# Reciprocals of the softmax sums, broadcast by four transfers per quad instead of one

## The chip, the cores and the metric

The kernel runs on one core of one Trainium2 chip. The metric is the device time of one execution in microseconds. Three runs of the kernel before gave 896.04, 896.61 and 898.95 us; the median is 896.61 us.

## What is computed

One transformer block over 2048 tokens of 512 columns, conditioned by a vector `c`: six rows of shift, scale and gate come out of `c`, then attention with 32 heads of 16 columns, then a gated feed-forward layer of 1792 columns.

```python
mod = (_silu(c) @ w_mod).reshape(c.shape[0], 6, 1, -1)          # sa, ca, ga, sb, cb, gb
h = _layernorm(x) * (1 + ca) + sa
qkv = (h @ wqkv) ...                                              # 32 heads, 16 columns each
scores = jnp.einsum('bhqd,bhkd->bhqk', q, k) * 16 ** (-0.5)
o = jnp.einsum('bhqk,bhkd->bhqd', _softmax(scores), v)
x = x + ga * (o @ wo)
h = _layernorm(x) * (1 + cb) + sb
x = x + gb * ((_gelu(h @ w_gate) * (h @ w_up)) @ w_down)
```

The softmax divides by a sum over the keys. The change touches only the path by which the reciprocals of these sums reach the vector engine.

## The kernel before

The kernel is written out by a recorder. The methods of `_Recorder` (`mm`, `act`, `tt`, `ts`, `dma` and so on) put each operation on one of five in-order queues: PE (matrix), ACT (scalar), DVE (vector), POOL, and SP, which issues nearly all transfers. `rec` (line 169) works out which semaphores an operation has to wait for, from the bytes that it reads and writes, and `emit` (line 381) writes the queues out. A planner (`stream`, line 1097) decides the order while recording. It keeps an own estimate of the times (`model`, line 246; a transfer there occupies SP for 450 ns) and always takes what its estimate says is ready. So the order of all five queues depends on the estimated cost of each operation: an edit that changes these costs changes the order of other work too.

**Attention.** The queries are cut into six sets (`SETS`, line 31): three of 512 queries, one of 256 and two of 128. The heads are taken four at a time; four heads of one set are called a quad here (a unit in the code), and there are eight quads for each set, except that the last two sets share their first five quads. PE computes scores into `ps_sc` (`qk`, line 1342), ACT takes their exponentials into `E`, one to three tiles of 512 columns in one instruction (line 1286), and PE multiplies them with the values into `ps_pv` (`pv_mms`, line 1354). The values have a 17th column of ones, so that the sum of the exponentials comes out as a 17th row of each head: a quad occupies rows 32j to 32j+16 of the 128, j from 0 to 3, with the sum in row 32j+16. Part of the exponentials is not computed on ACT: DVE makes them out of the scores with integer arithmetic, into `dreg` or `mreg` (line 1293), and four shifted copies of each (`shift_task`, line 1366). The planner decides which rounds go there (lines 1261 to 1275), four score tiles at a time.

**End of a quad.** `unit_end` (line 1388) copies `ps_pv` to `osb` (128 rows, 512, 256 or 128 columns, f32). Then a chain of steps follows: the four rows of sums go to DRAM (`scr_den`), come back spread over 128 rows (`den`), DVE takes the reciprocals (`rden`), these go to DRAM (`scr_rec`), and one transfer brings them back as `rb`, each head's row of reciprocals repeated over its 32 rows (line 1408). `fin2` (line 1411) multiplies `osb` by `rb` into `onorm`, which the output projection (`wo`) reads. Rows 32j+16 to 32j+31 of `wo` are zero, so that only rows 32j to 32j+15 of `onorm` count. Of the 43 quads' ends, 39 go through this chain; quads 6 and 7 of the last two sets take another way (`near_end`, line 845), by PE and a reciprocal on DVE.

**Steps and queues.** The steps of the chain form one task: the planner puts each step on its queue as soon as its estimate says that it can start, and the next step only after that. SP holds, besides these steps, the loads of the feed-forward weights (256 KB each, lines 897, 902 and 794 to 804) and the stores of the output. The feed-forward layer and the projections run between the attention work as side work (`plan`, line 1022), on PE, DVE and a little on ACT. PE also runs matmuls that only keep it busy (`ps_sc<-xs,ident` and `ps_mi<-xs,ident`, lines 1258 and 1330).

The prologue (line 496) loads the inputs, zeroes or fills some tiles on POOL and DVE, normalises the first four tiles of tokens and starts the attention.

Of the kernel before, what the change touches and what calls it, by code (L numbers as in the profile page):

```python
# [17 lines left out]
DH = 16  # L18
# [398 lines left out]
class _Kernel(_Recorder):  # L417
# [78 lines left out]
    def prologue(self):  # L496
        sp, act, pe, dve, pool = "sp", "act", "pe", "dve", "pool"
        xv = self.A_x.rearrange("b (t p) d -> p (b t) d", p=P)
        wmv = self.w_mod.rearrange("(a p) n -> p a n", p=P)
        wqv = self.A_wqkv.rearrange("(a p) (k n) -> p a k n", p=P, k=3)  # L500
        wq4 = self.wqkv.rearrange("p a (k n) -> p a k n", k=3)
        self.dma(sp, self.xs[:, 0:2, :], xv[:, 0:2, :], "x0")
        self.dma(act, self.crow[0:1, :], self.c, "c")
        self.dma(act, self.xs[:, 2:4, :], xv[:, 2:4, :], "x1")
        for i in range(2):
            self.dma(sp, self.wmod[:, :, D * i:D * i + D], wmv[:, :, D * i:D * i + D], "wm%d" % i)
        for k in (1, 0):
            self.dma(act, wq4[:, :, k, 0:P], wqv[:, :, k, 0:P], "wq%d" % k)
        self.dma(sp, self.xs[:, 4:8, :], xv[:, 4:8, :], "x2")
        self.dma(sp, wq4[:, :, 2, 0:P], wqv[:, :, 2, 0:P], "wq2")  # L510
        for i in range(2, 4):
            self.dma(sp, self.xs[:, 4 * i:4 * i + 4, :], xv[:, 4 * i:4 * i + 4, :], "x%d" % (i + 1))
        for k in range(3):
            self.dma(sp, wq4[:, :, k, P:D], wqv[:, :, k, P:D], "wr%d" % k)
        self.dma(sp, self.wmod[:, :, 1024:3072], wmv[:, :, 1024:3072], "wm2")

        self.memset(dve, self.warm, 0.0)
        self.memset(dve, self.ones, 1.0)
        self.memset(dve, self.pv[:, :], 0.0)
        self.memset(dve, self.scp[:, SC - 1, :], 0.0)  # L520
        self.warm_up(7)
        self.memset(pool, self.ident[:, :], 0.0)
        self.affine_select(self.ident[:, :], [[-1, P]], ALU.not_equal, 1.0, 0, 1)
        self.memset(pool, self.rm4, 1.0)
        self.affine_select(self.rm4, [[-32, 4]], ALU.is_ge, 0.0, -16, 1)
        self.affine_select(self.rm4, [[32, 4]], ALU.is_ge, 0.0, 31, -1)
        self.reduce(self.rm[:, 1:2], self.rm4, mybir.AxisListType.X, ALU.add)
        self.ts(dve, self.rm[:, 0:1], self.rm[:, 1:2], -1.0, 1.0, ALU.mult, ALU.add)
        self.memset(pool, self.vaug[:, :, :].rearrange("p t (h c) -> p t h c", c=VW)[:, :, :, DH:VW], 1.0)

        for dc in range(NDC):
            self.mm(self.scp[:, 0, dc:dc + 1], self.crow[0:1, P * dc:P * dc + P], self.ones[0:1, 0:1])
        self.act(self.tcol[:, :], self.scp[:, 0, 0:NDC], ACT.Tanh, scale=0.5)
        self.ln_stat(0)
        self.ln_stat(1)
        self.stt(self.tcol[:, :], self.tcol[:, :], 1.0, self.scp[:, 0, 0:NDC], ALU.add, ALU.mult)
        self.ts(dve, self.sc_bf[:, :], self.tcol[:, :], 0.5, None, ALU.mult)
        self.warm_up(6)
        self.mod_cols(self.scp[:, 1, 0:8], 0, range(4))
        self.warm_up(6)  # L540
        self.ln_stat(2)
        self.ln_stat(3)
        self.ln_rstd(0, 4)
        self.mod_cols(self.scp[:, 1, 0:8], 0, range(4, 8))
        self.warm_up(2)
        nb = self.nwt[:, 0:4]
        self.stt(nb, self.mv[:, 0:4, 0], -1.0, self.rstd[:, 0:4], ALU.mult, ALU.mult)
        for t in range(4):
            dst = self.tb1[:, 0, t, :]
            if t % 2 == 0:  # L550
                self.ln_norm(t, dst)
            else:
                self.act(dst, self.xs[:, t, :], ACT.Identity, bias=nb[:, t:t + 1], scale=self.rstd[:, t:t + 1])
        self.copy(dve, self.modA[:, :], self.scp[:, 1, 0:8])
        self.ts(dve, self.modA[:, 4:8], self.modA[:, 4:8], 1.0, None, ALU.add)
        pts = [self.scp[:, 2 + dc, :].bitcast(BF16)[:, 0:512] for dc in range(3)] + [self.mi[:, :].bitcast(BF16)[:, 0:512]]
        for t in range(4):
            for dc in range(NDC):
                self.transpose(pts[dc][:, P * t:P * t + P], self.tb1[:, 0, t, P * dc:P * dc + P], self.ident[:, :])
        for dc in range(NDC):  # L560
            self.modulate(dve if dc % 2 == 0 else act, self.hT[:, dc, 0:512], pts[dc], self.modA, dc)
        self.ln_stat(4)
        self.proj_q(0, 0, self.scp[:, 3, :], act)
        kb = self.scp[:, 4, :]
        self.proj(kb, 512, 0)
        for e in range(2):
            self.ts(dve, self.km[e][:, 0, 0:512], kb, self.rm[:, e:e + 1], None, ALU.mult)
        for t in range(5, 8):
            self.ln_stat(t)
# [818 lines left out]
    def unit_end(self, u, acc):  # L1388
        sets, qd, q0, W = u
        b, lo, hi = self.osb_span(u)  # L1390
        osb, rb = self.osb[:, lo:hi], self.rb[:, lo:hi]
        assert not self.blocked(u)
        self.copy("dve", osb, acc[:, 0:W])
        if sets[0] >= len(SETS) - 2 and len(sets) == 1 and qd >= 6:
            self.done(("osb", sets[0], qd))
            return
        self.live[u] = (lo, hi)
        m = 4 * W // P
        o = 8 if BCOL[sets[0]] else 0
        sem = b + 4 * (o > 0)  # L1400
        s1, s2 = self.scr1[b, P * o:P * o + 4 * W], self.scr2[b, P * o:P * o + 4 * W]
        den, rden = self.den[:, b, o:o + m], self.rden[:, b, o:o + m]
        steps = [
            ("sp", lambda: self.dma("sp", s1.rearrange("(j n) -> j n", j=4), self.osb[DH:P:32, lo:hi], "da%d" % sem)),
            ("sp", lambda: self.dma("sp", den, s1.rearrange("(p n) -> p n", p=P), "db%d" % sem)),
            lambda: self.recip(rden, den),
            ("sp", lambda: self.dma("sp", s2.rearrange("(p n) -> p n", p=P), rden, "dc%d" % sem)),
            ("sp", lambda: self.dma("sp", rb,
                                    s2.rearrange("(j o n) -> j o n", j=4, o=1).broadcast_to([4, 32, W]), "dd%d" % sem))]

        def fin2():
            c = OCOL[sets[0]]
            self.tt("dve", self.onorm[:, qd, c:c + W], osb, rb, ALU.mult)
            if self.probing is None:
                self.live.pop(u)
                for k in sets:
                    self.done(("onorm", k, qd))

        def free():
            c = OCOL[sets[0]]  # L1420
            return ("den", u) in self.have and all(
                ("wo", k) in self.have for k in range(sets[0]) if OCOL[k] < c + W and c < OCOL[k] + SETS[k][1])
        self.task(steps, ("den", u))
        self.task([fin2], None, free)
# [148 lines left out]
```

## Time and profile before

| what | value |
|---|---|
| median of three runs | 896.61 us (896.04 to 898.95) |
| the profiled execution | 895.94 us, span 894.1 us, mean granted clock 0.992 |
| busy, share of the span: PE, ACT, DVE, POOL | 91%, 94%, 76%, 0% |
| transfers | 47.64 MB, mean 53 GB/s |

The span runs from the first to the last instruction of the profile; the execution around it is 1.84 us longer. Engines are PE, ACT, DVE, POOL and SP as above, PEld the loading of weights into PE, and "SPq" SP's issuing of transfers. A row of the timeline gives the start and the duration in us, the engine, the line, the operation, what it writes and reads, how many such instructions, and in brackets how long the engine stood idle before it and what ended that. A row of the groups gives an instruction by its shape, its count, its busy time in us and the mean ns of one, and the idle time before it. A row of waits gives the waiting engine and its line, what it waited for, the total us, the times and the longest one. Most operations are recorded by a helper, so that their line is that of the helper; they are told apart by their tiles.

### The profile page before, as it was taken

Reading aid. Unit: us, or ns where it says so; the run is one execution under the profiler, and the core shown is the slowest. Engines: PE = TensorE matmul, PEld = TensorE weight load, DVE = VectorE, ACT = ScalarE, POOL = GpSimd, SP = SyncE. Lnnn points to the kernel's source line nnn. Section 1 sums busy time; section 2 is a strip of 40 time slices with the busy share of each in tenths; the row PEclk is TensorE's granted clock in tenths of the full one; section 3 lists DMA queues with packets and bytes.
Section 4 is the critical chain, followed back from the end, with each engine's and each line's share of the span. In section 5 each row is a group of like instructions: output and inputs, shape, how many; then the busy total and the mean of one; then the engine's idle time right before and its main releaser. Section 6 shows DMA issues by size and latency. Waiting matters only on the chain.

```text
span 894.1 us, 27778 instructions
## 1 busy us (share of the span) xinstructions
PE 811.9 (91%) x12637; PEld 284.9 (32%) x12642; DVE 680.8 (76%) x1288; ACT 843.9 (94%) x740; POOL 3.7 (0%) x11
## 2 busy tenths in 40 slices
PE   7899899989998998999999899999988889988887
PEld 3333232322222222223322222223433333344355
DVE  7745689988998888998888999989846672655264
ACT  5999999999999999999999999999989999999982
POOL 1000000000000000000000000000000000000000
PEclk9999999999999999999999999999999999999999
DMA  9000000000003101211003121110003321663300
GB/s 305 2 26 23 8 15 12 18 14 15 3 26 85 49 26 39 60 49 37 27 1 95 40 61 37 49 50 15 28 27 102 85 80 38 173 198 91 101 7 13
DMA packets 73115, 47.64 MB, mean 53 GB/s; under 512 B 15369, under 2 KB 69318, under 8 KB 72998
## 3 DMA queue, kind: packets, MB, share of 16 engines
q1 hardware_dynamic: 71668, 45.34, 17.2%
q8 instruction: 99, 1.62, 0.7%
q10 hardware_dynamic: 1330, 0.53, 0.2%
q14 instruction: 18, 0.15, 0.1%
HBM read 43.25 MB, written 2.61 MB: 51 GB/s over the span
## 4 chain that ended last, share of the span: by engine, by line
ACT 57%; PE 26%; DVE 8%; DMA 6%; issue 1%; SPq 0%; ACTq 0%; DVEq 0%
ACT E L324 55%; PE ps_mi L311 10%; PE ps_sc L311 10%; PE ps_pv L311 6%; DMA rb<-scr_rec 4%; ACT wreg L324 2%; DVE dreg L336 1%; DMA scr_rec<-rden 1%; DVE st L364 1%; DVE onorm L328 1%; DMA xs<-in_A_x_dram 1%; DVE osb L345 1%; DVE mreg L336 0%; DVE wreg L328 0%; DMA mreg<-in_B_w_gate_dram 0%
## 5 line engine op out<-in xcount | busy, mean ns | idle before, releaser
L324 ACT ACTIVATE E<-ps_sc 128x1536 bf16<-128x1536 f32 (+2 forms) x698 | 817.1, 1330 | 31.9 <-PE ps_sc L311 30.6
L311 PE MATMUL ps_sc<-qT,kmo 32*128 32x512 bf16 (+2 forms) x1408 | 177.4, 324 | 10.8 <-ACT E L324 8.5
L311 PE MATMUL ps_sc<-qT,kme 32*128 32x512 bf16 (+2 forms) x1344 | 171.9, 333 | 14.3 <-ACT E L324 10.8
L311 PE MATMUL ps_pv<-E,vaug 128*17 128x512 bf16 (+2 forms) x2392 | 172.9, 323 | 3.5 <-DVE osb L345 2.2
L336 DVE TENSOR_SCALAR dreg<-ps_sc 128x512 uint16<-128x512 f32 x184 | 126.5, 690 | 32.3 <-PE ps_sc L311 30.1
L311 PE MATMUL ps_mi<-wreg,mreg 128*32 128x512 bf16 (+2 forms) x1920 | 119.9, 350 | 17.7 <-DVE wreg L341 10.1
L336 DVE TENSOR_SCALAR mreg<-dreg 128x2048 uint16<-128x2048 uint16 x184 | 121.0, 685 | 2.4 <-PE ps_pv L311 2.2
L311 PE MATMUL ps_pv<-mreg,vs 128*17 128x512 bf16 (+1 forms) x1184 | 95.2, 363 | 2.6 <-DVE mreg L336 2.3
L311 PEld LDWEIGHTS ps_sc<-qT,kme 32*128 32x128 bf16 x1344 | 44.5, 91 | 136.1 <-ACT E L324 90.3
L311 PEld LDWEIGHTS ps_sc<-qT,kmo 32*128 32x128 bf16 x1408 | 47.2, 92 | 122.4 <-ACT E L324 83.1
L311 PEld LDWEIGHTS ps_pv<-E,vaug 128*17 128x17 bf16 x2392 | 53.2, 89 | 88.8 <-issue 61.3
L336 DVE TENSOR_SCALAR mreg<-ps_sc 128x512 uint16<-128x512 f32 x88 | 60.6, 690 | 14.6 <-PE ps_sc L311 13.3
L311 PEld LDWEIGHTS ps_mi<-wreg,mreg 128*32 128x32 bf16 x1920 | 41.6, 96 | 72.5 <-issue 23.3
L336 DVE TENSOR_SCALAR mreg<-mreg 128x2048 uint16<-128x2048 uint16 x88 | 57.6, 685 | 0.1
L311 PE MATMUL ps_sc<-xs,ident 128*32 128x512 bf16 x445 | 38.1, 385 | 15.8 <-ACT E L324 14.7
L345 DVE CAST wreg<-ps_mi 128x512 bf16<-128x512 f32 x51 | 35.1, 688 | 21.3 <-PE ps_mi L311 20.8
L341 DVE SCALAR_TENSOR_TENSOR wreg<-wreg,ps_mi 128x512 bf16<-128x512 bf16 x51 | 34.9, 684 | 13.7 <-PE ps_mi L311 11.2
L328 DVE TENSOR_TENSOR onorm<-osb,rb 128x512 bf16<-128x512 f32 (+2 forms) x43 | 23.6, 551 | 27.7 <-DMA rb<-scr_rec 27.5
L311 PE MATMUL ps_mi<-wo,onorm 128*32 128x512 bf16 x480 | 37.8, 407 | 2.4 <-DVE onorm L328 2.0
L311 PE MATMUL ps_mi<-hreg,wreg 128*32 128x512 bf16 x480 | 39.4, 383 | 0.6 <-DVE qT L336 0.4
L345 DVE COPY osb<-ps_pv 128x512 f32<-128x512 f32 (+2 forms) x42 | 22.9, 546 | 21.2 <-PE ps_pv L311 21.1
L311 PEld LDWEIGHTS ps_pv<-mreg,vs 128*17 128x17 bf16 x1184 | 27.3, 89 | 33.7 <-DVE mreg L336 16.1
(133 smaller groups left out, 578.7 us busy)
## 6 DMA issues: line engine op xcount, KB each, us to landing
mreg<-in_B_w_up_dram SPq DMA_DIRECT2D x32, 256.0 KB, 3.6
mreg<-in_B_w_gate_dram SPq DMA_DIRECT2D x28, 256.0 KB, 3.6
rb<-scr_rec SPq DMA_DIRECT2D x24, 256.0 KB
mreg<-in_B_w_down_dram SPq DMA_DIRECT2D x16, 256.0 KB, 2.6
dreg<-in_B_w_down_dram SPq DMA_DIRECT2D x12, 256.0 KB, 4.8
mreg<-in_w_mod_dram SPq DMA_DIRECT2D x1, 2048.0 KB, 12.4
out_dram<-xs SPq DMA_DIRECT2D x16, 128.0 KB, 1.7
rb<-scr_rec SPq DMA_DIRECT2D x13, 128.0 KB
```

The costliest lines, as they stand in the source:

```text
L311: return self.rec("pe", lambda e: e.matmul(out, lhsT, rhs, start=start, stop=stop, tile_position=tp), [lhsT, rhs], [out], cost=(n, int(rhs ...
L324: return self.rec("act", lambda e: e.activation(out, in_, func, scale=scale, **kw), rd, wr, cost=self.cost("act", out, [in_], "act"))
L328: return self.rec(eng, lambda e: e.tensor_tensor(out, a, b, op), [a, b], [out], cost=self.cost(eng, out, [a, b], "tt"))
L336: return self.rec(eng, lambda e: e.tensor_scalar(out, a, s1, s2, **kw), rd, [out], cost=self.cost(eng, out, [a], "ts"))
L341: return self.rec("dve", lambda e: e.scalar_tensor_tensor(out, a, s, b, op0=op0, op1=op1), rd, [out], cost=self.cost("dve", out, [a, b], " ...
L345: return self.rec(eng, lambda e: e.tensor_copy(out, in_), [in_], [out], cost=self.cost(eng, out, [in_], "ts"))
L364: return self.rec("dve", lambda e: e.bn_stats(out, in_), [in_], [out], cost=self.cost("dve", out, [in_], "bn"))
```

## The change

The one transfer that fills `rb` for a quad becomes four, one for each head, each a step of its own with a semaphore of its own. Each repeats the head's row of reciprocals over 16 rows, not 32. The other rows of `rb` are never written by a transfer any more; POOL zeroes the whole of `rb` once in the prologue.

```diff
         self.memset(pool, self.vaug[:, :, :].rearrange("p t (h c) -> p t h c", c=VW)[:, :, :, DH:VW], 1.0)
+        self.memset(pool, self.rb[:, :], 0.0)
...
             lambda: self.recip(rden, den),
             ("sp", lambda: self.dma("sp", s2.rearrange("(p n) -> p n", p=P), rden, "dc%d" % sem)),
-            ("sp", lambda: self.dma("sp", rb,
-                                    s2.rearrange("(j o n) -> j o n", j=4, o=1).broadcast_to([4, 32, W]), "dd%d" % sem))]
+            ]
+        steps += [("sp", lambda j=j: self.dma(
+            "sp", self.rb[32 * j:32 * j + DH, lo:hi],
+            s2[W * j:W * j + W].rearrange("(o n) -> o n", o=1).broadcast_to([DH, W]), "dd%d%d" % (sem, j)))
+            for j in range(4)]
```

The planner records the changed steps with their own estimated costs, and the order of the queues comes out differently. Up to about the first 70% of PE's queue only few neighbours change places. After that, from the last quads of the third set on, the order is new in many places, and the planner gives two more groups of four score tiles to DVE: ACT has 384 exponentials of three tiles and 308 of two (before 392 and 300), DVE makes 280 tiles with their 280 shifted copies (before 272 and 272), and PE has 416 instead of 444 filling matmuls into `ps_sc`, 80 more and 16 fewer matmuls of 256 columns into `ps_pv`. SP issues 156 transfers into `rb` instead of 39. Each `onorm` multiplication waits for four semaphores of transfers instead of one.

## The prediction

> **What bounds the kernel now.** I read the page first, then the list of waits, then the groups by shape, then the timeline around the waits for `rb`.
>
> ```profile
> span 894.1 us, 27778 instructions
> PE 811.9 (91%) x12637; PEld 284.9 (32%) x12642; DVE 680.8 (76%) x1288; ACT 843.9 (94%) x740; POOL 3.7 (0%) x11
> ACT 57%; PE 26%; DVE 8%; DMA 6%; issue 1%; SPq 0%; ACTq 0%; DVEq 0%
> ```
>
> ```profile
> ACT E L324 <- PE ps_sc L311: 30.6, 40, 2.1
> DVE onorm L328 <- DMA rb<-scr_rec: 27.5, 14, 5.6
> SPq L374 <- DVE osb L345: 236.9, 32, 22.5
> ```
>
> ACT is busy 843.9 of 894.1 us and holds 57% of the chain that ended last. So two things can shorten the kernel: less work on ACT, and less of its 50 us of idle time. DVE stands 27.5 us in 14 waits for the transfer that the change replaces. DVE itself has 213 us of idle time, so such a wait matters only where it passes on to PE and from there to ACT. The timeline shows three places where it does (start, duration, idle time before in brackets):
>
> ```profile
> 482.22 0.69 DVE L328 TENSOR_TENSOR onorm<-osb,rb 128x512 bf16<-128x512 f32 x1 [1.51 <-DMA rb<-scr_rec]
> 486.10 9.33 ACT L324 ACTIVATE E<-ps_sc 128x1536 bf16<-128x1536 f32 x8 [1.75 <-PE ps_sc L311]
> ```
>
> ```profile
> 628.57 0.53 SPq L374 DMA_DIRECT2D rb<-scr_rec  x1
> 633.52 0.69 DVE L328 TENSOR_TENSOR onorm<-osb,rb 128x512 bf16<-128x512 f32 x1 [2.10 <-DMA rb<-scr_rec]
> 635.29 1.45 ACT L324 ACTIVATE E<-ps_sc 128x1536 bf16<-128x1536 f32 x1 [0.62 <-PE ps_sc L311]
> 637.48 2.12 ACT L324 ACTIVATE E<-ps_sc 128x1024 bf16<-128x1024 f32 x2 [0.74 <-PE ps_sc L311]
> ```
>
> ```profile
> 651.98 0.31 DVE L348 RECIPROCAL rden<-den 128x16 f32<-128x16 f32 x2
> 654.60 1.13 SPq L374 DMA_DIRECT2D rb<-scr_rec  x2
> 659.63 0.69 DVE L328 TENSOR_TENSOR onorm<-osb,rb 128x512 bf16<-128x512 f32 x1 [5.59 <-DMA rb<-scr_rec]
> 661.58 1.45 ACT L324 ACTIVATE E<-ps_sc 128x1536 bf16<-128x1536 f32 x1 [1.28 <-PE ps_sc L311]
> 663.93 1.45 ACT L324 ACTIVATE E<-ps_sc 128x1536 bf16<-128x1536 f32 x1 [0.89 <-PE ps_sc L311]
> 666.10 7.08 ACT L324 ACTIVATE E<-ps_sc 128x1536 bf16<-128x1536 f32 x5 [0.72 <-PE ps_sc L311]
> ```
>
> Within a few microseconds after 9.2 us of DVE waits (1.51 + 2.10 + 5.59), ACT stands idle 6.0 us (1.75 + 0.62 + 0.74 + 1.28 + 0.89 + 0.72). That is 0.65 us of ACT for each microsecond of wait, and 6.0 us is what these three places can give.
>
> **The change part by part.**
>
> *The landing.* Today a 512-wide quad's `rb` is there 4.95 us after its issue (628.57 to 633.52). The narrower ones are:
>
> ```profile
> 839.81 0.55 SPq L374 DMA_DIRECT2D rb<-scr_rec  x1
> 843.03 0.42 DVE L328 TENSOR_TENSOR onorm<-osb,rb 128x256 bf16<-128x256 f32 x1 [1.80 <-DMA rb<-scr_rec]
> 843.21 0.55 SPq L374 DMA_DIRECT2D rb<-scr_rec  x1
> 845.95 0.29 DVE L328 TENSOR_TENSOR onorm<-osb,rb 128x128 bf16<-128x128 f32 x1 [1.31 <-DMA rb<-scr_rec]
> ```
>
> That is 3.22 us for 128 KB and 2.74 us for 64 KB. From 128 to 256 KB it grows by 1.73 us, so about 2 us are fixed. The row of one stretch in which a 256 KB transfer runs says why the rest is slow:
>
> ```profile
> 81.00:82.00 1.00, 0.85 (x18) 0.28 (x16) 0.99 (x6) 1.00 (x2) 0.00 (x0) 1.00 0.26 100
> ```
>
> The transfer engines are busy 0.26 (the last column but one) and move 100 GB/s: about four of sixteen at work. The Trainium skill, "DMA: Bandwidth & Descriptors", section "Rules for kernel authors", says that a leading broadcast dimension of fewer than sixteen copies confines a transfer to as many engines; the trace agrees with four, and by that rule the 16-row transfers run on all sixteen. The same section says to coalesce small transfers, since under 64 KB one mostly pays overhead: by the first rule the total is the forecast below, by the second it is that of the second rival.
>
> The four new transfers of a 512-wide quad hold 32 KB each. Their issue is bounded by SP's rows, and the last one's landing by the smallest load and the smallest `rb` now:
>
> ```profile
> L374 SPq DMA_DIRECT2D scr_rec<-rden x39: 319/338/927, 75.4 to 863.0; - x39
> L374 SPq DMA_DIRECT2D rb<-scr_rec x39: 522/522/568, 79.4 to 864.7; - x39
> den<-scr_den SPq DMA_DIRECT2D x24, 8.0 KB, 1.6
> ```
>
> Issue: 0.34 to 0.52 us each (medians); I take 0.40, nearer the row that is spread over many partitions in one plain dimension like the new ones. Landing of the last: 1.6 us (8 KB) to 2.74 us (64 KB); I take 1.9. From the first issue to the last landing this is 3 x 0.40 + 1.9 = 3.1 us, between 3 x 0.34 + 1.6 = 2.6 and 3 x 0.52 + 2.74 = 4.3. So 512-wide quads gain 1.85 us (0.65 to 2.35), 256-wide ones 0.1 (a loss of 1.1 to a gain of 0.6), and 128-wide ones lose 0.4.
>
> *The moved multiplication.* The planner's estimate of the four transfers is longer than that of the one, and so it places `onorm` later on DVE. In the changed order the multiplication of 482.22 stands behind two more normalisations, that of 633.52 behind some ten more instructions, and that of 659.63 behind eleven others that follow the reciprocal of its quad, 7 us at the 0.65 us of the groups below, while `rb` should be there 5.7 us after that reciprocal (2.6 to its issue, 651.98 to 654.60, and 3.1). With the shorter landing all three waits should be gone. Queued behind such a wait are DVE's score tiles, which PE needs to free `ps_sc`. Of the 6.0 us of ACT I count 5.0 as gained, since PE, busy 91% with its fillers, takes a little of it back; the bounds are 0 and 8.1 (6.0, and 0.65 of the remaining 3.3 us of 512-wide waits in the row below). A loss here is the second rival.
>
> *Work moved from ACT to DVE.* The groups by shape:
>
> ```profile
> L324 ACT ACTIVATE E<-ps_sc 128x1536 bf16<-128x1536 f32 x392 | 556.4, 1522 | 17.8 <-PE ps_sc L311 16.7
> L324 ACT ACTIVATE E<-ps_sc 128x1024 bf16<-128x1024 f32 x300 | 302.1, 1096 | 5.5 <-PE ps_sc L311 5.2
> L336 DVE TENSOR_SCALAR dreg<-ps_sc 128x512 uint16<-128x512 f32 x184 | 126.5, 690 | 32.3 <-PE ps_sc L311 30.1
> L336 DVE TENSOR_SCALAR mreg<-dreg 128x2048 uint16<-128x2048 uint16 x184 | 121.0, 685 | 2.4 <-PE ps_pv L311 2.2
> L328 DVE TENSOR_TENSOR onorm<-osb,rb 128x512 bf16<-128x512 f32 x24 | 16.5, 686 | 12.6 <-DMA rb<-scr_rec 12.5
> L328 DVE TENSOR_TENSOR onorm<-osb,rb 128x256 bf16<-128x256 f32 x13 | 5.4, 422 | 13.7 <-DMA rb<-scr_rec 13.7
> ```
>
> Eight of ACT's instructions shrink from three tiles to two: 8 x (556.4/392 - 302.1/300) = 8 x 0.412 = 3.3 us less on the engine that holds most of the chain. DVE gets 8 x (126.5/184 + 121.0/184) = 10.8 us more. Both groups lie in the stretch of the fourth set:
>
> ```profile
> sum 100.00, PE 90.89 PEld 33.04 DVE 58.78 ACT 99.94 POOL 0.00; mean PE 18.18 PEld 6.61 DVE 11.76 ACT 19.99 POOL 0.00
> ```
>
> Between 680 and 780 us ACT is busy 99.94 of 100 and DVE 58.78, so DVE's 10.8 us are covered and ACT's 3.3 us count in full. PE has little to spare there (90.89). Its share follows from these rows:
>
> ```profile
> L311 PE MATMUL ps_sc<-xs,ident 128*32 128x512 bf16 x444 | 37.7, 385 | 15.8 <-ACT E L324 14.7
> L311 PE MATMUL ps_pv<-mreg,vs 128*17 128x256 bf16 x192 | 8.2, 273 | 0.2 <-DVE mreg L336 0.2
> ```
>
> 64 more value matmuls of 256 columns (80 more, 16 fewer) at 8.2/192 are 2.7 us, 28 fewer fillers at 37.7/444 are 2.4: 0.3 us more, nothing.
>
> *Three more semaphores for each `onorm`.* 117 waits that DVE has to read. No row shows one; below nothing is excluded, since only waits are added. The nearest rows are two small instructions in the prologue, of which the second waits for the first:
>
> ```profile
> 8.20 0.16 DVE L328 TENSOR_TENSOR nwt<-rstd 128x4 f32<-128x4 f32 x1
> 8.39 0.16 DVE L328 TENSOR_TENSOR nwt<-nwt,nwx 128x4 f32<-128x4 f32 x1
> ```
>
> They start 0.19 us apart, so one wait is 0 to 0.19 us, and I take the 0.03 between the end and the start: 3.5 us on DVE, of which I count 0.5, as most of DVE's time is covered.
>
> *SP.* 39 x (4 x 0.40 - 0.52) = 42 us more issuing (32 to 61). SP waits 237 us for `osb` alone, so it has room; loads queued behind come about 1.1 us later each time. The feed-forward layer starts its loads ahead of their use, which covers this; without that cover each quad would cost up to 1.1 us, and that is part of the second rival's price.
>
> *POOL's memset.* The first `rb` transfer is issued at 79.4, so POOL has time. What could hurt is DVE in the prologue:
>
> ```profile
> 2.03 2.28 POOL L352 MEMSET vaug<- 128x512 bf16 x1
> 9.46 0.73 DVE L336 TENSOR_SCALAR dreg<-xs,mv,rstd 128x512 bf16<-128x512 bf16 x2
> ```
>
> The new memset starts at 4.3 and has twice the elements and four times the bytes: 4.6 to 9.1 us, to 8.9 or 13.4. I take 0 for it, as it most likely ends before 9.46 (the element count is the nearer row); a loss is the third rival.
>
> *A new order.* Other moves late in the queues go both ways. I add 1.0 us, between 0 and the 6.0 that the three places now cost.
>
> Sum: -3.3 - 5.0 + 0.5 + 1.0 = -6.8. The profiled execution took 895.94 us, 1.84 us around its span of 894.1, so 889.1; the median of the runs lies 0.67 above the profiled one, which gives 889.8, rounded to **890**. With the bounds of the stall it is 895.94 + 0.67 - 3.3 - 8.1 = 885.2 at best, and 894.8 when the stall gives nothing.
>
> **The rivals.**
>
> *Nothing is left of it.* ACT waits for PE, not for DVE (30.6 us in 40 waits), and PE is near full. Then the idle time that goes here returns a few tiles later, and the shorter ACT work is lost the same way: 896.6. A stretch in which `onorm` never waits for `rb` shows that it can (PE's busy time, then PEld, DVE and ACT):
>
> ```profile
> 420.00:440.00 20.00, 20.00 (x272) 6.01 (x264) 15.73 (x27) 18.35 (x17) 0.00 (x0) 1.00 0.06 16
> ```
>
> PE is full there, and ACT idle for 1.65 us of 20. Against it: in the three places ACT's gaps follow DVE's waits.
>
> *The issues make it slower.* If each new transfer costs SP 0.52 us, and its landing the 2.74 us, the set lands after 4.3 us. The fifteen narrow quads are then 1.1 us later each, 16.5 us of DVE waits, 10.7 us of ACT by the ratio of 0.65; the three wide places get 0.65 us each, 1.3 us of ACT; ACT's work falls by 3.3: 896.61 + 10.7 - 1.3 - 3.3 = 902.7. It decides once an issue takes about 0.5 us and `onorm`'s 256-wide group waits clearly longer than 13.7 us. Against it: the planner also moves these multiplications later, and from 680 to 780 us, where narrow quads end, ACT is full all the same.
>
> *POOL holds DVE in the prologue.* The Trainium skill, "SBUF — State Buffer", section "Who interferes with whom", says that POOL and a DVE instruction in a two-port mode shut each other out for a whole instruction. As a mechanism here: the memset runs to 13.4, the normalisation at 9.46 waits up to 3.9 us, and everything behind it too: 893.7. While `vaug` was filled, no large DVE instruction of that kind ran, so the trace neither shows nor excludes it.
>
> *The new order is worse.* The recomputed last quarter may meet its own gaps; at twice the three places' 6.0 us, less the gains, it is 896.61 + 12.0 - 8.3 = 900.3.
>
> **How the numbers follow.** About 0.3% (2.7 us) is what a measurement of this kernel can tell from no change. Forecast 0.56; nothing left 0.18; issues 0.13; POOL 0.05; new order 0.08. Faster (below 893.9): 0.53 of the forecast, 0.03 of POOL, 0.02 of the second: 0.58. Slower (above 899.3): 0.13, 0.06 of the order, 0.01 of the second: 0.20. The rest, 0.22, is the same. The range from 884 to 902 takes in the bounds and most of the slower cases; the forecast's own is 885 to 895.
>
> **What would show it.** Right: `rb` lands about 3 us after its first issue at every width; the waits of `onorm` fall from 27.5 us to under 15, the 512-wide ones to under 4; ACT is busy near 840.6 us and DVE near 691; SP's issue of a new transfer takes 0.34 to 0.45 us. Wrong: an issue of 0.5 us or more, 256-wide waits above 13.7 us, ACT's idle time unchanged at 50 us, or a first exponential clearly later than in the profile of before.

## The result and the profile after

The changed kernel takes 885.79 us (median of four runs, 883.84 to 888.02), the kernel before in the same measurement 897.78 us. The ratio is 0.9864 with a 95% interval of 0.9826 to 0.9902. Two further measurements beside the experiments below gave 0.9853 [0.982, 0.9887] and 0.985 [0.9815, 0.9885]. So the kernel became 1.4 to 1.5% faster, 12 to 13.5 us, where 6.8 had been forecast. Times are compared only within one measurement, and between measurements only ratios, as the median of the kernel before moved between 897.78 and 901.05 us. One run of e1 (922.13 us, at a mean granted clock of 0.85) is left out of every figure.

The page of the changed kernel (profiled execution 883.84 us):

```profile
span 882.1 us, 28068 instructions
PE 807.7 (92%) x12673; PEld 285.1 (32%) x12678; DVE 690.4 (78%) x1304; ACT 839.5 (95%) x740; POOL 4.5 (1%) x12
ACT 60%; PE 31%; DVE 6%; DMA 1%; issue 1%; SPq 0%; ACTq 0%; DVEq 0%
```

ACT is busy 839.5 us (843.9 before), and so idle 42.6 us of the span (50.2 before). Less work gives 4.4 us and less idle time 7.6; together they are the 12.0 us by which the span fell. Transfers (DMA) went from 6% of the last chain to 1%. The list of waits (us in total, times, longest):

```profile
ACT E L324 <- PE ps_sc L311: 23.5, 32, 2.3
DVE onorm L328 <- DMA rb<-scr_rec: 4.7, 7, 1.3
```

The 27.5 us for which DVE stood before the reciprocals are 4.7, and ACT's waits for PE fell from 30.6 to 23.5. The groups by shape:

```profile
L324 ACT ACTIVATE E<-ps_sc 128x1536 bf16<-128x1536 f32 x384 | 545.4, 1516 | 10.4 <-PE ps_sc L311 9.4
L324 ACT ACTIVATE E<-ps_sc 128x1024 bf16<-128x1024 f32 x308 | 309.8, 1097 | 5.7 <-PE ps_sc L311 5.5
L328 DVE TENSOR_TENSOR onorm<-osb,rb 128x512 bf16<-128x512 f32 x24 | 16.4, 683 | 0.8 <-DMA rb<-scr_rec 0.8
L328 DVE TENSOR_TENSOR onorm<-osb,rb 128x256 bf16<-128x256 f32 x13 | 5.5, 421 | 2.9 <-DMA rb<-scr_rec 2.8
L328 DVE TENSOR_TENSOR onorm<-osb,rb 128x128 bf16<-128x128 f32 x6 | 1.7, 282 | 1.2 <-DMA rb<-scr_rec 1.2
```

Nearly all of the idle time that ACT got rid of stood in front of the three-tile exponentials: 17.8 us before, 10.4 now. The new transfers, first by their issues on SP (shortest, median and longest in ns), then by their landing, and one set of four on the timeline:

```profile
L374 SPq DMA_DIRECT2D rb<-scr_rec x156: 317/420/1857, 81.7 to 853.8; - x156
DMA to landing us min/median/max: 1.5/1.8/4.3
```

```profile
155.52 1.71 SPq L374 DMA_DIRECT2D rb<-scr_rec  x4
```

Four issues take 1.71 us, so the last one starts 1.29 us after the first and lands 1.8 us later (the median): 3.1 us. Of the 39 sets, 33 take 1.71 to 1.92 us to issue, and six take 2.22 to 3.29.

**Where the time came from, and what the forecast had not seen.** In the view by windows of 4 us (span of the window; busy time and count of PE, PEld, DVE, ACT, POOL; granted clock; share and rate of the transfers), these are two of the stretches in which the kernel before waited:

```profile
480.00:484.00 4.00, 2.78 (x33) 0.76 (x25) 2.49 (x8) 4.00 (x4) 0.00 (x0) 1.00 0.67 154
484.00:488.00 4.00, 3.91 (x31) 1.72 (x31) 2.60 (x6) 2.25 (x3) 0.00 (x0) 0.57 0.52 155
656.00:660.00 4.00, 1.81 (x44) 0.59 (x36) 0.36 (x1) 4.00 (x4) 0.00 (x0) 1.00 0.26 92
660.00:664.00 4.00, 3.58 (x44) 1.06 (x48) 2.36 (x6) 1.83 (x3) 0.00 (x0) 0.72 0.05 11
664.00:668.00 4.00, 4.00 (x68) 1.46 (x64) 1.99 (x4) 3.28 (x3) 0.00 (x0) 0.85 0.09 33
```

and the same five in the changed kernel:

```profile
480.00:484.00 4.00, 3.08 (x41) 0.78 (x41) 3.97 (x13) 4.00 (x4) 0.00 (x0) 1.00 0.65 155
484.00:488.00 4.00, 3.65 (x48) 1.59 (x48) 3.34 (x9) 4.00 (x4) 0.00 (x0) 1.00 0.47 147
656.00:660.00 4.00, 4.00 (x88) 1.62 (x88) 2.38 (x6) 3.95 (x4) 0.00 (x0) 1.00 0.05 6
660.00:664.00 4.00, 4.00 (x98) 1.80 (x86) 2.65 (x6) 3.87 (x4) 0.00 (x0) 1.00 0.09 21
664.00:668.00 4.00, 3.03 (x66) 1.10 (x58) 3.51 (x14) 4.00 (x4) 0.00 (x0) 1.00 0.01 3
```

Before, DVE's wait first thins out PE (1.81 of 4 us at 656). ACT is busy 4.00 while DVE waits and 1.83 afterwards, and the granted clock falls as well; such a fall is called a dip here. Narrower windows at the second place show which comes first:

```profile
661.00:661.50 0.50, 0.50 (x10) 0.11 (x6) 0.50 (x1) 0.00 (x0) 0.00 (x0) 1.00 0.00 0
661.50:662.00 0.50, 0.46 (x11) 0.28 (x12) 0.47 (x3) 0.42 (x1) 0.00 (x0) 0.77 0.12 33
662.00:662.50 0.50, 0.50 (x12) 0.17 (x6) 0.50 (x2) 0.50 (x1) 0.00 (x0) 0.50 0.00 0
```

ACT's gap of 1.28 us ends at 661.58 with the clock still full, and the dip runs from 661.77 to 665.18. At 484 the dip (484.27 to 487.69) holds the whole gap of 1.75 us. Of the 6.0 us of ACT's gaps at the prediction's three places, 2.64 us (1.75 and 0.89) lie inside a dip, 0.72 begins 0.2 us after one, and 2.64 (0.62, 0.74 and 1.28) lie at the full clock: there the wait passes on to ACT by itself. In a dip PE looks full (3.58, 4.00 above) because its instructions take longer. The third dip of the kernel before shows that on one group: 32 matmuls of the feed-forward layer, ahead of the dip and in it:

```profile
806.64 1.06 PE L311 MATMUL ps_mi<-wreg,mreg 128*32 128x256 bf16 x32 [1.34 <-DVE wreg L341]
808.49 1.89 PE L311 MATMUL ps_mi<-wreg,mreg 128*32 128x256 bf16 x32 [0.47 <-DVE wreg L345]
```

That dip follows a 256-wide quad's wait (1.57 us at 804.90), and in the stretch from 800 to 820 us ACT was busy 17.52 us before:

```profile
800.00:820.00 20.00, 16.92 (x400) 8.88 (x392) 12.20 (x26) 17.52 (x16) 0.00 (x0) 0.91 0.50 141
```

and 19.84 in the changed kernel, which is ahead by then, so that not quite the same work stands there:

```profile
800.00:820.00 20.00, 18.22 (x491) 10.24 (x486) 12.06 (x28) 19.84 (x18) 0.00 (x0) 1.00 0.43 126
```

Each dip takes the same: (1 - 0.57) x 4 us at 484, and (1 - 0.72) x 4 + (1 - 0.85) x 4 at 660, are 1.72 us of full clock both, that is 3.4 us at half. The Trainium skill, "TensorE: Matmul & The Clock Gate", section "Part 1: The HAM clock gate", says that the matrix array falls to half its clock after a window of about 3.4 us in which it was idle and gets the full clock back after a busy one; the length agrees. That the window must be idle does not: PE was busy 2.29 of the 3.41 us right ahead of the dip at 484.27.

### The profile page after: what moved, and what is told of

It is laid out like the page before. It is cut to its first block, busy times and chain, and to the rows that moved or that the text cites. A ratio compares the mean times of both kernels' runs of the same rounds, so it can differ in the third digit from the quotient of the medians.

```text
span 882.1 us, 28068 instructions
## 1 busy us (share of the span) xinstructions
PE 807.7 (92%) x12673; PEld 285.1 (32%) x12678; DVE 690.4 (78%) x1304; ACT 839.5 (95%) x740; POOL 4.5 (1%) x12
## 4 chain that ended last, share of the span: by engine, by line
ACT 60%; PE 31%; DVE 6%; DMA 1%; issue 1%; SPq 0%; ACTq 0%; DVEq 0%
ACT E L324 58%; PE ps_mi L311 12%; PE ps_sc L311 12%; PE ps_pv L311 7%; ACT wreg L324 2%; DVE dreg L336 1%; DVE mreg L336 1%; DVE wreg L341 1%; DMA xs<-in_A_x_dram 1%; DVE st L364 0%; DVE osb L345 0%; SPq L374 0%; DMA rb<-scr_rec 0%; DMA mreg<-in_B_w_gate_dram 0%; DVE kme L336 0%
## 5 line engine op out<-in xcount | busy, mean ns | idle before, releaser
L324 ACT ACTIVATE E<-ps_sc 128x1024 bf16<-128x1024 f32 (+2 forms) x698 | 813.1, 1323 | 24.8 <-PE ps_sc L311 23.5
L311 PE MATMUL ps_sc<-qT,kmo 32*128 32x512 bf16 (+2 forms) x1408 | 178.6, 323 | 11.6 <-ACT E L324 8.7
L311 PE MATMUL ps_sc<-qT,kme 32*128 32x512 bf16 (+2 forms) x1344 | 173.1, 332 | 13.5 <-ACT E L324 10.6
L336 DVE TENSOR_SCALAR dreg<-ps_sc 128x512 uint16<-128x512 f32 x188 | 129.3, 690 | 34.6 <-PE ps_sc L311 32.4
L336 DVE TENSOR_SCALAR mreg<-dreg 128x2048 uint16<-128x2048 uint16 x188 | 123.4, 683 | 2.9 <-PE ps_pv L311 2.7
L311 PE MATMUL ps_pv<-mreg,vs 128*17 128x512 bf16 (+1 forms) x1248 | 97.2, 358 | 2.4 <-DVE mreg L336 2.1
L336 DVE TENSOR_SCALAR mreg<-ps_sc 128x512 uint16<-128x512 f32 x92 | 63.4, 691 | 16.3 <-PE ps_sc L311 15.0
L336 DVE TENSOR_SCALAR mreg<-mreg 128x2048 uint16<-128x2048 uint16 x92 | 60.0, 683 | 0.1
L311 PE MATMUL ps_sc<-xs,ident 128*32 128x512 bf16 x417 | 36.2, 390 | 14.3 <-ACT E L324 13.3
L328 DVE TENSOR_TENSOR wreg<-wreg 128x1024 bf16<-128x1024 bf16 (+1 forms) x60 | 35.9, 605 | 0.6
L311 PE MATMUL ps_mi<-wo,onorm 128*32 128x512 bf16 x480 | 35.1, 382 | 1.1 <-DVE onorm L328 0.9
L311 PE MATMUL ps_mi<-mreg,hreg 128*32 128x512 bf16 x448 | 34.9, 383 | 0.0
```

The costliest lines, as they stand in the source:

```text
L311: return self.rec("pe", lambda e: e.matmul(out, lhsT, rhs, start=start, stop=stop, tile_position=tp), [lhsT, rhs], [out], cost=(n, int(rhs ...
L324: return self.rec("act", lambda e: e.activation(out, in_, func, scale=scale, **kw), rd, wr, cost=self.cost("act", out, [in_], "act"))
L328: return self.rec(eng, lambda e: e.tensor_tensor(out, a, b, op), [a, b], [out], cost=self.cost(eng, out, [a, b], "tt"))
L336: return self.rec(eng, lambda e: e.tensor_scalar(out, a, s1, s2, **kw), rd, [out], cost=self.cost(eng, out, [a], "ts"))
```

## The experiments

Each row gives the median, the ratio to the kernel before on the same chip with its 95% interval, the wait of `onorm` for `rb` in the profiled execution, and the granted clock as a mean over the compared runs. Kernels between two rules ran on one chip, and the kernel before beside them.

| kernel | median us | ratio | wait us | clock |
|---|---|---|---|---|
| before | 901.05 | 1 | | 0.986 |
| e1_new_transfers_old_order | 892.60 | 0.9902 [0.9869, 0.9935] | 22.4 | 0.992 |
| e2_old_transfer_new_order | 888.08 | 0.9849 [0.9818, 0.9881] | 7.7 | 0.994 |
| e3_rows32_no_memset | 885.09 | 0.9819 [0.9788, 0.985] | 8.6 | 0.996 |
| e4_old_transfer_true_estimate | 888.86 | 0.9862 [0.983, 0.9894] | 8.6 | 0.990 |
| --- | | | | |
| before | 899.96 | 1 | | 0.987 |
| after_again (the changed kernel) | 886.47 | 0.9853 [0.982, 0.9887] | 6.3 | 0.994 |
| e5_68_groups | 888.52 | 0.987 [0.9836, 0.9903] | 4.1 | 0.996 |
| e6_eight_transfers | 889.28 | 0.9881 [0.985, 0.9913] | 9.4 | 0.995 |
| e7_memset_late | 884.61 | 0.9831 [0.98, 0.9862] | 7.0 | 0.997 |
| --- | | | | |
| before | 899.62 | 1 | | 0.989 |
| after_third (the changed kernel) | 886.69 | 0.985 [0.9815, 0.9885] | 7.1 | 0.996 |
| e8_rows32_again | 888.96 | 0.9861 [0.9822, 0.9899] | 7.7 | 0.995 |
| e9_rows32_later | 885.45 | 0.984 [0.9808, 0.9873] | 5.6 | 0.996 |

### The faster transfers alone: e1

The kernel before with its order of every queue; only what the one step on SP issues is new, and the memset on POOL is there.

```diff
-            ("sp", lambda: self.dma("sp", rb,
-                                    s2.rearrange("(j o n) -> j o n", j=4, o=1).broadcast_to([4, 32, W]), "dd%d" % sem))]
+            ("sp", lambda: self.four(sem, W, s2, lo, hi))]
...
+    def four(self, sem, W, s2, lo, hi):
+        rb = self.rb[:, lo:hi]
+
+        def fn(e):
+            return [e.dma_start(self.rb[32 * j:32 * j + DH, lo:hi],
+                                s2[W * j:W * j + W].rearrange("(o n) -> o n", o=1).broadcast_to([DH, W])) for j in range(4)]
+        fn.parts = 4
+        return self.rec("sp", fn, [s2], [rb], dma="dd%d" % sem, cost=(128 * W * 4, W * 4))
```

> The kernel before with its order of all queues kept, but the four new transfers (and POOL's memset) in place of the one; the planner still believes in one old transfer, and the four share one semaphore. Theory A (the new order is the main cause, the faster landing helps little): the wide waits of onorm shrink by about 1.85 us each (1.51, 2.10 and 5.59 become 0, 0.3 and 3.7), the narrow ones stay, so onorm waits about 19 us instead of 27.5 and the time is about 894 us, ratio 0.995 to 0.998. Theory B (the faster landing is the main cause): onorm waits under 10 us and the time is 885 to 889 us, ratio about 0.988.

Measured: 0.9902 [0.9869, 0.9935]. The groups of `onorm` by shape in e1:

```profile
L328 DVE TENSOR_TENSOR onorm<-osb,rb 128x512 bf16<-128x512 f32 x24 | 16.4, 684 | 4.5 <-DMA rb<-scr_rec 4.5
L328 DVE TENSOR_TENSOR onorm<-osb,rb 128x256 bf16<-128x256 f32 x13 | 5.4, 421 | 14.4 <-DMA rb<-scr_rec 14.4
L328 DVE TENSOR_TENSOR onorm<-osb,rb 128x128 bf16<-128x128 f32 x6 | 1.7, 290 | 3.7 <-DMA rb<-scr_rec 3.5
```

The 512-wide quads, whose transfer became 1.85 us faster, wait 4.5 us instead of 12.5; the 256-wide ones wait as long as before (14.4 against 13.7) and the 128-wide ones longer, as the landings of the prediction have it. So four small transfers pay only where the one was large; alone they are worth 1%. Neither theory has it whole: the waits fall only to 22.4 us, near the 19 of theory A, but the time falls by some 8 us, where theory A had 2 to 4. The two profiled spans differ by 5.2 us (894.1 and 888.9); over all runs the mean granted clock is 0.992 against 0.986.

### The later multiplication alone: e2 and e4

e2 has the changed kernel's order of every queue, and the old transfer: the first three of the four steps issue nothing and the fourth issues the one transfer to 128 rows (the expectation speaks of the place of the first).

```diff
-        steps += [("sp", lambda j=j: self.dma(
-            "sp", self.rb[32 * j:32 * j + DH, lo:hi],
-            s2[W * j:W * j + W].rearrange("(o n) -> o n", o=1).broadcast_to([DH, W]), "dd%d%d" % (sem, j)))
-            for j in range(4)]
+        steps += [("sp", lambda j=j: self.quarter(j, sem, W, s2, lo, hi)) for j in range(4)]
...
+    def quarter(self, j, sem, W, s2, lo, hi):
+        def fn(e):
+            return e.dma_start(self.rb[:, lo:hi], s2.rearrange("(j o n) -> j o n", j=4, o=1).broadcast_to([4, 32, W]))
...
+        if op is not None and j < 3:
+            op.fn = None
```

> The order of all queues of the changed kernel, but the one old transfer to 128 rows, issued in the place of the first of the four. Theory A (order): the planner has put onorm late enough that even the old landing of 4.95 us (512 wide) and 3.22 us (256 wide) mostly fits; onorm waits 5 to 10 us and the time is 886 to 889 us, ratio 0.988 to 0.991. Theory B (landing): the waits come back, over 15 us, and the time is 892 us or more, ratio above 0.994.

e4 is the kernel before, with the planner told how long its transfer really takes; the planner then makes an order of its own.

```diff
+    def told(self, W, op):
+        if op is not None:
+            op.t1 += {512: 2230, 256: 910, 128: 640}[W]
...
-            ("sp", lambda: self.dma("sp", rb,
-                                    s2.rearrange("(j o n) -> j o n", j=4, o=1).broadcast_to([4, 32, W]), "dd%d" % sem))]
+            ("sp", lambda: self.told(W, self.dma(
+                "sp", rb, s2.rearrange("(j o n) -> j o n", j=4, o=1).broadcast_to([4, 32, W]), "dd%d" % sem)))]
```

> The kernel before with its one transfer, but the planner is told its measured landing (4.95, 3.22 and 2.74 us for 512, 256 and 128 columns); it plans a third order. Theory A (order, that is a true estimate): onorm's waits fall under 8 us without any change of the transfer, and the time is 885 to 890 us. Theory B (landing): no gain beyond 2 us, 895 us or more. A time in between or worse with short waits says that a newly made order is worth several us either way by itself.

Measured: e2 0.9849 [0.9818, 0.9881], e4 0.9862 [0.983, 0.9894]. Both have the old transfer, whose 512-wide and 256-wide groups read in e2 (line numbers are one higher there)

```profile
L329 DVE TENSOR_TENSOR onorm<-osb,rb 128x512 bf16<-128x512 f32 x24 | 16.4, 685 | 4.9 <-DMA rb<-scr_rec 4.9
L329 DVE TENSOR_TENSOR onorm<-osb,rb 128x256 bf16<-128x256 f32 x13 | 5.4, 419 | 1.8 <-DMA rb<-scr_rec 1.8
```

and in e4

```profile
L328 DVE TENSOR_TENSOR onorm<-osb,rb 128x512 bf16<-128x512 f32 x24 | 16.3, 681 | 0.0
L328 DVE TENSOR_TENSOR onorm<-osb,rb 128x256 bf16<-128x256 f32 x13 | 5.5, 420 | 8.3 <-DMA rb<-scr_rec 8.3
```

In e4 a transfer as slow as before is never waited for by a 512-wide multiplication. So the wait of the kernel before came from the place of `onorm` in DVE's queue, set by an estimate that was 2.2 us too short for the wide quads, as much as from the transfer. Either kernel alone has the ratio of the changed kernel (0.985 to 0.9864), so most of the gain is the order's. Whether anything is left for the faster landing once the order is right is not settled: on the same chip e3 below, with four transfers, was faster than e2 and e4 by 2.8 and 3.9 us in the means of their runs (each ± 2.3, a 95% interval from the scatter of the runs), but its second measurement has a ratio of 0.9861. The two are in large part substitutes: the transfers alone give 1.0%, the order alone 1.4 to 1.5%, and both together (the changed kernel, e3 and e8) 1.4 to 1.8%, not their sum of 2.4.

### 32 rows instead of 16: e3 and e8

The changed kernel with 32 rows for each transfer and no memset; `size` keeps the planner's estimate and with it the order.

```diff
-        self.memset(pool, self.rb[:, :], 0.0)
...
-            "sp", self.rb[32 * j:32 * j + DH, lo:hi],
-            s2[W * j:W * j + W].rearrange("(o n) -> o n", o=1).broadcast_to([DH, W]), "dd%d%d" % (sem, j)))
+            "sp", self.rb[32 * j:32 * j + 32, lo:hi],
+            s2[W * j:W * j + W].rearrange("(o n) -> o n", o=1).broadcast_to([32, W]), "dd%d%d" % (sem, j), size=DH * W * 4))
```

> The changed kernel with 32 rows in each of the four transfers instead of 16, and no memset by POOL; the order of PE, DVE, ACT and SP is the changed kernel's. If the gain comes from transfers that run on all engines at once and from the order, halving the rows is worth little: landing of one transfer 1.8 to 2.0 us, time within 1 us of the changed kernel, 885 to 887 us. If halving the bytes matters: 888 us or more. If POOL's memset delays the prologue: the first exponential starts about 1.5 us earlier than in the profile of the changed kernel and the time falls by as much.

> Four transfers of 32 rows instead of 16, without the memset, in the changed kernel's order (the same kernel as e3_rows32_no_memset, here beside the changed kernel on one chip). Theory one, writing only the 16 used rows is worth nothing, the four-way split does it all: within 1.5 us of the changed kernel. Rival, half the bytes matter: the later landing (2.1 us where 16 rows take 1.8) lengthens 39 waits by up to 0.3 us, 12 us on DVE, and the time by 3 us or more.

> The changed kernel once more, as the measure for the two others. A ratio to the kernel before of 0.983 to 0.989, as in the two measurements so far; waits of onorm for rb of 4 to 7 us.

Measured: 0.9819 [0.9788, 0.985] and, for the same kernel on another chip beside the changed one, 0.9861 [0.9822, 0.9899], where the changed kernel has 0.985. The landing grows from 1.8 to 2.1 us and the waits from 7.1 to 7.7. Halving the rows is worth nothing that these runs can tell, in either direction. The medians of e8 and after_third differ by 2.3 us, more than the 1.5 that was expected, but e8's six runs lie at 884.2 and 884.5, with a granted clock of 0.998, and at 888.9 to 889.4, with 0.992 to 0.994. The two profiles of this kernel show what such a difference costs. In the windows of e8

```profile
88.00:92.00 4.00, 4.00 (x42) 1.04 (x38) 1.83 (x5) 3.44 (x4) 0.00 (x0) 0.70 0.28 70
92.00:96.00 4.00, 4.00 (x29) 0.91 (x29) 2.76 (x5) 2.96 (x4) 0.00 (x0) 0.50 0.00 0
96.00:100.00 4.00, 4.00 (x37) 0.58 (x25) 2.38 (x5) 3.03 (x3) 0.00 (x0) 0.52 0.01 2
```

and of e3, whose instructions are the same and stand some 1.7 us earlier,

```profile
88.00:92.00 4.00, 3.66 (x43) 0.88 (x36) 3.27 (x6) 4.00 (x6) 0.00 (x0) 1.00 0.12 32
92.00:96.00 4.00, 3.44 (x44) 0.91 (x48) 3.90 (x7) 4.00 (x4) 0.00 (x0) 1.00 0.01 2
96.00:100.00 4.00, 3.64 (x95) 1.51 (x96) 4.00 (x7) 3.99 (x5) 0.00 (x0) 1.00 0.01 4
```

the one execution lost (0.30 + 0.50 + 0.48) x 4 = 5.1 us of clock and the other none. ACT was busy 9.43 us in the one and 11.99 in the other: half a microsecond of ACT for each microsecond of clock that is lost. This is the price of one long dip, without any change in the kernel.

### Later still: e9

The kernel of e8, with the planner told a later landing for the narrow quads.

```diff
+    def told(self, j, W, op):
+        if op is not None and j == 3:
+            op.t1 += {512: 0, 256: 600, 128: 600}[W]
...
-        steps += [("sp", lambda j=j: self.dma(
+        steps += [("sp", lambda j=j: self.told(j, W, self.dma(
```

> As e8_rows32_again, but the planner is told that the last of the four transfers lands 0.6 us later for the 256-wide and 128-wide quads, whose multiplications still wait 8 us in all; the order changes only late in the kernel. Theory one, the remaining waits count at the 0.65 us of ACT per us of wait that the prediction used: they fall to 2 us or less and the time by up to 4 us against e8_rows32_again. Rival, these waits lie beside work that ends later anyway: within 1.5 us of e8_rows32_again.

Measured: 0.984 [0.9808, 0.9873]; the 256-wide waits fall from 5.4 to 3.0 us, and all waits to 5.6, not to the 2 that were expected. The median is 3.5 us below e8's, the interval too wide to count that. It is inconclusive.

### The work moved from ACT to DVE: e5

```diff
-                    elif (cand and self.quad_free and ...
+                    elif (getattr(self, "groups", 0) < 68 and cand and self.quad_free and ...
...
+                        self.groups = getattr(self, "groups", 0) + 1
```

> The changed kernel, except that the planner may place only 68 groups of four score tiles on DVE, as many as in the kernel before; so ACT gets back 8 score tiles (392 instructions of three tiles, 300 of two). Theory one, ACT's work counts in full: ACT is busy about 843 us and the kernel takes 3.3 us more than the changed kernel, some 0.4%. Rival, ACT's share there is hidden by PE being full: within 1 us of the changed kernel.

Measured: 888.52 against 886.47 us for the changed kernel, 2.05 us more. ACT's three-tile group is back at

```profile
L324 ACT ACTIVATE E<-ps_sc 128x1536 bf16<-128x1536 f32 x392 | 556.2, 1513 | 11.4 <-PE ps_sc L311 10.2
```

The intervals, 0.987 [0.9836, 0.9903] and 0.9853 [0.982, 0.9887], overlap (1.5 us ± 2.1 in the means of the two): the sign and the size fit theory one better than the rival, but they don't settle it.

### Twice the transfers: e6

The changed kernel's order; each step issues two transfers of 8 rows.

```diff
+        def fn(e):
+            return [e.dma_start(self.rb[32 * j + 8 * i:32 * j + 8 * i + 8, lo:hi],
+                                src.rearrange("(o n) -> o n", o=1).broadcast_to([8, W])) for i in range(2)]
...
+        steps += [("sp", lambda j=j: self.halves(j, sem, W, s2, lo, hi)) for j in range(4)]
```

> The order of every queue as in the changed kernel, but each of its four steps issues two transfers of 8 rows instead of one of 16: eight transfers for a quad. By the measured 0.42 us for one issue the set takes 8 x 0.42 = 3.4 us to issue and lands about 1.7 us later than in the changed kernel (some 4.8 us after its first issue). Theory one, the later place of the multiplication covers it: the waits of onorm for rb rise from 4.7 us to 8 to 15 us, most of it in the 256-wide groups, and the time by at most 2 us. Rival, SP's issuing and the landing set the end: 39 sets x 1.7 us = 66 us more of DVE's waits, of which a good part reaches ACT, and the time rises by 5 us or more.

Measured: 889.28 us, 2.8 us more than the changed kernel, with waits of 9.4 us. One of its sets on SP:

```profile
629.43 2.69 SPq L385 DMA_DIRECT2D rb<-scr_rec  x8
```

Eight issues take 2.69 us, not 3.4, as an issue of 8 rows takes 0.30 us, so this adds only 1 us to each set. That 39 x 0.98 = 38 us of additional issuing cost 2.8 us says that most of it is covered, as theory one had it; whether its bound of 2 us was too low the runs can't tell (2.5 us ± 2.2 in the means). The Trainium skill, "DMA: Bandwidth & Descriptors", section "Rules for kernel authors", would have small transfers coalesced; the step from four to eight agrees with it in sign, the step from one to four (e1 against the kernel before), which also halves the bytes, goes the other way.

### The memset in the prologue: e7 and after_again

The first profile of the changed kernel has its first exponential at 17.00 us, the kernel before at 15.53, and the prediction had named that as a sign against it. POOL's two fills in the changed kernel's timeline:

```profile
2.03 2.27 POOL L352 MEMSET vaug<- 128x512 bf16 x1
3.90 1.25 POOL L352 MEMSET rb<- 128x1024 f32 x1
```

The memset is over at 5.15 us, well ahead of the normalisation at 9.46 in the prediction's rival. e7 moves it about 58 us back in POOL's queue.

```diff
-        self.memset(pool, self.rb[:, :], 0.0)
...
         self.affine_select(selv, [[-32, 4], [0, 32]], ALU.not_equal, 1.0, -16, 1)
+        self.memset("pool", self.rb[:, :], 0.0)
```

> The order of every queue as in the changed kernel, but POOL's memset of rb stands later in POOL's own queue, behind its next instruction (about 60 us), still ahead of the first rb transfer. Theory one, the memset in the prologue is what made the first exponential come 1 to 2 us later: it comes near 15.5 us, and the time is 1 to 1.5 us below the changed kernel's. Rival, the later start has another cause: first exponential at 16.5 us or later, the same time as the changed kernel.

> The changed kernel once more, beside the three others, so that they are compared with it on one chip. Its first profile had its first exponential at 17.00 us (before: 15.53) and a granted clock of 0.54 from 12 to 14 us. If POOL's memset in the prologue is the cause, the first exponential comes at 16.5 us or later again; if it is chance of one execution, it may come near 15.5. Time against before: a ratio of 0.983 to 0.990, as in the first measurement.

Measured: e7, without the memset in the prologue, starts its first exponential late,

```profile
17.15 1.45 ACT L324 ACTIVATE E<-ps_sc 128x1536 bf16<-128x1536 f32 x1 [2.36 <-PE ps_sc L311]
```

and the changed kernel in its second profile, with the memset, early:

```profile
15.60 1.45 ACT L324 ACTIVATE E<-ps_sc 128x1536 bf16<-128x1536 f32 x1 [1.51 <-PE ps_sc L311]
```

So the memset is not the cause; theory one falls. All thirteen profiles say the same: with the memset in the prologue the first exponential starts at 15.47 and 15.60 us in two and at 16.53 to 17.44 in five, without it at 15.48 to 15.61 in three and at 17.15 to 17.63 in three. (e7's median is 1.9 us lower than the changed kernel's beside it, with overlapping intervals, and its profile shows that it isn't by an earlier start.) In e7's windows the granted clock is

```profile
12.00:14.00 2.00, 1.67 (x5) 0.63 (x6) 1.17 (x3) 0.90 (x2) 0.00 (x0) 0.60 1.10 341
14.00:16.00 2.00, 1.87 (x5) 0.41 (x3) 0.09 (x1) 0.60 (x1) 0.00 (x0) 0.55 1.10 327
```

The same dip stands in the first profile of the changed kernel (0.54 and 0.61 in these windows), and not in that of the kernel before (1.00 and 1.00). Of the eight late starts, six have a dip that begins between 11 and 14 us; e1 and e8 have none, and in e8 PE waits 2.79 us for the load of `w_mod` instead. So far as these profiles show, whether an execution starts late is chance; one profile's 1.5 us there say nothing of the change.

## Why the prediction was right, point by point

The time, 885.79 us, lies inside the range of 884 to 902, the direction is that of the likeliest case, and the sum of -6.8 us was some 5 us too small. The gain itself, 12.0, 13.5 and 12.9 us in the three measurements, is beyond the best that the sum's bounds allowed (896.61 to 885.2, that is 11.4). That the time still lies inside the forecast's own 885 to 895 is partly luck: the forecast starts from 896.61 us, and all later medians of the kernel before are higher (897.78 to 901.05).

*The landing* came as worked out: 3.1 us from the first issue to the last landing, 0.42 us for an issue (0.40 taken) and 1.8 for the landing (1.9 taken). SP's issuing grew by 54 us (42 forecast, 32 to 61), from 20.7 to 74.2 over the 39 sets. The old transfer at 152.84 us took at most 0.27 of the sixteen transfer engines in any quarter of a microsecond; those of e3, with 32 rows, took 0.96 over half a microsecond at 155, so they were not confined to four.

*The waits* went as forecast: 4.7 us in all (under 15), 0.8 for the wide quads (under 4). But "with the shorter landing all three waits should be gone" named one cause of two. Of the 12.5 us of 512-wide waits, e1 leaves 4.5 with the new landing and the old order, e2 leaves 4.9 with the old landing and the new order, and e4 leaves none with the old landing and an order of its own. Over all widths it is the order that carries the effect (7.7 us left in e2, 22.4 in e1), as the sentence ahead of it, on the planner's longer estimate, had it.

*The stall term* is the one that was mis-sized. ACT's idle time fell by 7.6 us, while -5.0 for the stall, +0.5 for the semaphores and +1.0 for the order are -3.5. Three things were missed. First, the places: the three wide waits gave some 6.0 us, not 5.0 (ACT is busy 97.29 instead of 94.79 of the 100 us from 400 on, and 98.58 instead of 95.05 from 600 on), and the sum took them alone, while a stretch behind a 256-wide wait (800 to 820 us) gave 2.3 us more of ACT (19.84 against 17.52). Second, the ratio of 0.65 us of ACT for each microsecond of wait was read as the wait passing on; that holds for 2.64 of the 6.0 us, while as much lies in dips and 0.72 just behind one. Third, the kernel before meets more such dips in most of its runs than in the profiled one: its granted clock was 0.992 there, and 0.987 as a mean over its 33 runs beside the experiments. Spans times one less the clock are 11.6 us lost in a run of the kernel before and 4.4 in one of the changed kernel (mean of 16). At 0.5 us of time for each, as between e8 and e3, that is 3.6 of the 13.9 us by which the mean spans differ; the slope of span against lost clock, fitted within the runs of each of the two, is 0.7 and 0.6, which would make it 4.3 to 5. That the dips follow the stalls is argued from the windows and from e1, which with the same order and shorter stalls has 0.992 against 0.986; no run forced a dip, so this part of the gain is not shown.

*ACT's shorter work* was right: the two groups of exponentials went from 858.5 to 855.2 us, the 3.3 of the forecast; the rest of the 4.4 us by which ACT's busy time fell is in neither group. What it is worth in time is 2.05 us by e5, in which the order of the last part changes too.

*DVE's and PE's terms.* DVE got 9.6 us (10.8 forecast), and ACT stays full where most of it went (79.77 of the 80 us from 700 on, 79.94 before), so it is covered. The three additional semaphores do not show: idle time ahead of `onorm` that is not a wait for the transfers is 0.1 us or less in each group by shape, before and after (12.6 and 12.5, 0.8 and 0.8 for the 512-wide one). PE's busy time fell by 4.2 us where 0.3 more was forecast: matmuls in a dip are longer (1.89 against 1.06 us above), and the profile of the kernel before lost 7.4 us of clock, that of the changed one 3.4.

*The memset* takes 1.25 us, well under the 4.6 to 9.1 estimated from the strided fill of `vaug`; that row was the wrong neighbour for a contiguous tile. The 0 that was taken for it stands, and its rival falls with e7.

*The new order* was entered as +1.0, a cost. e2, the new order with the old transfer, gains 13 us, so the order as a whole is the main source of the gain. It holds the later multiplications and ACT's shorter work, though, which the sum has as terms of their own; what the other moves cost or gain by themselves no run shows.

*The rivals.* "Nothing is left of it" falls, as ACT's idle time went. "The issues make it slower" needed 0.5 us for an issue and more than 13.7 us of 256-wide waits, and there are 0.42 and 2.8; e6 with eight issues for a quad is still faster than the kernel before. "The new order is worse" falls with e2.

No kernel tried beats the changed one by more than its interval: e3, e7 and e9 lie at 0.982 to 0.984, and e3's second measurement at 0.986.

## What to carry to other kernels

Where an instruction waits for a transfer, look first at where the instruction stands in its queue and at the estimate that put it there: here the right estimate for the old transfer (e4) gained 1.4%, the faster transfer with its new order 1.4 to 1.5%. A faster part and a later use can be substitutes, so cost them as alternatives before you add them. When a stall thins out PE, read the granted clock of the next microseconds before pricing it, and compare kernels by the clock of all their runs, since the profiled one may have met fewer dips than the rest.

## What was not expected of the hardware

- The granted clock goes to half for 3.41 us or a multiple of it: of the 27 dips that lie whole in the thirteen profiles, 22 last 3.41 us, three 6.83 and two 10.24. Within a profile their starts lie whole multiples of 3.413 us apart (484.27, 661.77, 808.54 and 849.50 in the kernel before: 52, 43 and 12 of them; the nine profiles with two or more dips agree). So the clock is set anew in fixed periods, which lie elsewhere in each execution, and whether a thin stretch fills one period or is cut in two can differ from run to run.
- PE need not be idle for a dip: in the period ahead of one it was busy 1.22 to 2.78 of 3.41 us. Its busy time alone does not decide: in the kernel before, periods with 2.21 and 2.29 us (from 846.08 and 480.86 on) were followed by a dip, and periods with 2.13 and 2.19 (from 866.56 and 794.88 on) were not. What else decides stays open.
- An issue on SP takes 0.30 us for a transfer to 8 rows, 0.42 for 16 rows and for 32 alike, and 0.52 for the old one to 4 x 32.
- POOL fills 128x1024 f32 in 1.25 us in one contiguous piece (0.95 in e7, later in the kernel) and takes 2.27 us for 128x512 bf16 in strides. The two rows overlap by 0.4 us, so POOL's spans are rough.
